# Ten more no-ops ahead of the second long visit of TensorE's stream, four fewer ahead of the fifth, and TensorE's idle operand cleared as VectorE's first instruction

## The chip, the cores and the metric

The kernel runs on one core of a Trainium2 chip. Times are device microseconds of one execution of the whole kernel, medians over several runs. A profile's "span" is shorter by about 2 us, since it counts only from the first to the last of the program's own instructions.

## The reference, cut to what matters

```python
x = A_x                                   # 2048 x 512, bf16
xn = _layernorm(x)                        # per row
# sliding-window attention: 32 heads of 16, window of 256 keys
# (qkv projection, scores, softmax, values, output projection)
attn = _A_ref(xn, A_wqkv, A_wo)
# bilinear gated unit, width 1792
glu = ((xn @ w_gate) * (xn @ w_up)) @ w_down
return x + attn + glu
```

## The kernel before

TensorE does nearly all of it in one stream that was ordered by hand: big matmuls of 512 columns ("filler": projections, gate, up, down) stand between small groups for the attention. A score group multiplies 32-row pieces of K and Q. A values group multiplies many small pieces of the probabilities with V; where two such groups follow each other, the text speaks of a "long visit". There are five of them, of 384 instructions each (192 weight loads and 192 matmuls).

Three pieces of the kernel matter here. The start, where VectorE clears an operand on which TensorE then idles, to get its clock up before the real work comes:

```python
# ... the DMA issues of x and of the weights stand above
warm = const.tile([128, 1], F32, name="warm")
nc.vector.memset(warm[:], 0.0)
nc.scalar.activation(out=warm[:], in_=warm[:], func=ACT.Exp)
self.idle = const.tile([128, 128], BF16, name="idle")
nc.vector.memset(self.idle[:], 0.0)
self.keep_busy(40)              # 40 matmuls idle x idle, result unused
```

The stock of no-ops, which is filled at given steps and used up three at a time:

```python
PADS = {27: 110, 57: 150}       # step: no-ops added to the stock
# ... in run(), at each step g
self.pads += PADS.get(g, 0)
# ... in fill(), after each piece of filler (two matmuls of 512 columns)
for _ in range(min(3, self.pads)):
    self.nc.tensor.nop("pad", nofuse=True)
    self.pads -= 1
```

And the values group:

```python
for i, (P, col, m, q, n) in enumerate(todo):
    for par in range(2):
        for e in range(4):
            # ... v is a 64 x 32 piece of V or of its half-swapped copy VS
            nc.tensor.matmul(accs[par][32 * e:32 * e + 32, q:q + n], lhsT=v,
                             rhs=P[rows, e, col:col + n], ...)
```

The softmax here doesn't subtract the row's maximum and nothing guards it: scores larger than these inputs give would overflow.

## Time and profile before

| | before |
|---|---|
| time, median of the first 3 runs | 263.57 us (263.21 to 263.72) |
| time, median of the 6 runs known later | 263.34 us (263.21 to 263.72) |
| span of the profiled execution | 261.2 us |
| TensorE's share of the chain that ended last | 98% |
| each of the five long visits in that chain | 2.40 us |
| first idle matmul, first projection matmul | 1.07 us, 6.67 us |

How to read it: TensorE's share of the chain says which engine sets the end, and the lengths of equal pieces of work say whether that engine is ever held up. The lines themselves stand in the prediction.

### The profile page before, as it was taken

The page shows a single profiled execution, that of the slowest core. Times are in us where ns is not written, and L with a number is a line of the kernel's source. Part 1 is how long each engine was busy: PE and PEld are TensorE (multiplying, and loading weights), DVE is VectorE, ACT ScalarE, POOL GpSimd, SP SyncE. Part 2 cuts the span into 40 slices and gives each one's busy share as a digit, 9 for nine tenths or more (in the row PEclk, how much of TensorE's full clock was granted, in tenths as well). Part 3 has the DMA queues.
Part 4 walks back from the last instruction along what each step waited for, and adds up shares of the span by engine and source line. Part 5 has one row for each costly group of instructions (what it writes and reads, how often), then busy time and mean ns, then how long its engine had stood idle before and what let it go on. Part 6 is the DMA issues. An engine that isn't in the chain of part 4 may idle for free.

```text
span 261.2 us, 7718 instructions
## 1 busy us (share of the span) xinstructions
PE 255.8 (98%) x3154; PEld 118.0 (45%) x3170; DVE 179.5 (69%) x357; ACT 176.4 (68%) x143; POOL 116.0 (44%) x278
## 2 busy tenths in 40 slices
PE   8999999999999999999999999999999999999995
PEld 8444444444344544444544454344544445444453
DVE  6787888779846597557974769767795235977344
ACT  3477688888757776678775567767787546787600
POOL 6225342425457644333457644544443451464600
PEclk9999999999999999999999999999999999999999
DMA  6999910120012300002001310001000100000002
GB/s 193 379 350 341 286 30 20 24 48 1 3 37 46 83 3 1 3 0 48 3 3 40 84 43 3 0 1 29 23 3 0 42 24 20 5 0 3 1 3 83
DMA packets 19427, 15.05 MB, mean 58 GB/s; under 512 B 7360, under 2 KB 19392, under 8 KB 19392
## 3 DMA queue, kind: packets, MB, share of 16 engines
q1 hardware_dynamic: 18848, 14.26, 18.6%
q8 instruction: 26, 0.43, 0.7%
q10 hardware_dynamic: 544, 0.30, 0.4%
q14 instruction: 9, 0.07, 0.1%
HBM read 9.70 MB, written 2.10 MB: 45 GB/s over the span
## 4 chain that ended last, share of the span: by engine, by line
PE 98%; issue 1%; DVE 0%
PE gp L399 19%; PE up L410 19%; PE psd L432 17%; PE qkp L255 11%; PE S L317 10%; PE acc L370 7%; PE vp L243 5%; PE psd L438 5%; PE L L432 2%; PE wps L131 2%; PE L L438 1%; PE xTp L213 0%; PE L L370 0%; DVE x L448 0%; DVE idle L95 0%
## 5 line engine op out<-in xcount | busy, mean ns | idle before, releaser
L323 ACT ACTIVATE P<-S 128x2048 bf16<-128x2048 f32 x75 | 140.7, 1876 | 49.6 <-PE S L317 41.0
L162 POOL TENSOR_SCALAR_AFFINE_SELECT P<-P 64x256 bf16<-64x256 bf16 x224 | 99.7, 445 | 123.7 <-ACT P L323 108.6
L399 PE MATMUL gp<-xnT,Wg 128*128 128x512 bf16 x224 | 60.1, 380 | 0.0
L410 PE MATMUL up<-xnT,Wu 128*128 128x512 bf16 x224 | 59.1, 380 | 0.0
L415 DVE TENSOR_TENSOR hT<-up,gsb 128x512 bf16<-128x512 f32 x56 | 38.3, 684 | 18.3 <-PE up L410 13.1
L432 PE MATMUL psd<-Wd,hT 128*128 128x512 bf16 (+1 forms) x202 | 46.9, 369 | 0.8 <-issue 0.6
L347 DVE TENSOR_TENSOR P<-P,diag 128x512 bf16<-128x512 bf16 (+1 forms) x75 | 29.6, 394 | 5.9 <-ACT P L323 5.9
L432 PEld LDWEIGHTS <-hT 128*128 128x128 bf16 x238 | 21.3, 98 | 25.3 <-issue 3.5
L410 PEld LDWEIGHTS <-Wu 128*128 128x128 bf16 x224 | 20.4, 98 | 25.6 <-issue 3.3
L399 PEld LDWEIGHTS <-Wg 128*128 128x128 bf16 x224 | 20.3, 98 | 25.3 <-issue 3.3
L317 PE MATMUL S<-Q,K 32*128 32x320 bf16 (+4 forms) x720 | 29.8, 254 | 0.1
L255 PE MATMUL qkp<-xnT,Wqkv 128*128 128x512 bf16 x128 | 29.9, 380 | 0.0
L234 ACT ACTIVATE gsb<-gp 128x512 bf16<-128x512 f32 x38 | 22.3, 596 | 7.7 <-PE gp L399 6.9
L317 PEld LDWEIGHTS <-K 32*128 32x128 bf16 x720 | 10.3, 92 | 30.7 <-issue 30.3
L376 DVE STREAM_TRANSPOSE at<-acc 128x512 f32<-128x512 f32 x30 | 19.1, 688 | 6.5 <-PE acc L370 6.4
L448 DVE TENSOR_TENSOR x<-psd,x 128x512 bf16<-128x512 f32 (+1 forms) x15 | 9.7, 655 | 15.7 <-PE psd L438 15.7
L255 PEld LDWEIGHTS <-Wqkv 128*128 128x128 bf16 x128 | 11.7, 98 | 14.7 <-issue 1.8
L370 PE MATMUL acc<-P,VS 64*32 64x320 bf16 (+4 forms) x672 | 17.7, 253 | 0.0
L370 PE MATMUL acc<-P,V 64*32 64x320 bf16 (+4 forms) x672 | 17.5, 253 | 0.0
L370 PEld LDWEIGHTS <-V 64*32 64x32 bf16 x720 | 15.1, 91 | 2.3 <-issue 1.7
L243 PE MATMUL vp<-Wqkv,xnT 128*128 128x512 bf16 x60 | 14.9, 380 | 0.3 <-issue 0.2
L370 PEld LDWEIGHTS <-VS 64*32 64x32 bf16 x720 | 14.7, 91 | 0.6 <-issue 0.2
(54 smaller groups left out, 180.5 us busy)
## 6 DMA issues: line engine op xcount, KB each, us to landing
out_dram<-x SPq DMA_DIRECT2D x15, 128.0 KB, 1.8
Wg<-in_B_w_gate_dram SPq DMA_DIRECT2D x2, 896.0 KB, 11.2
Wu<-in_B_w_up_dram SPq DMA_DIRECT2D x2, 896.0 KB, 12.6
Wd<-in_B_w_down_dram SPq DMA_DIRECT2D x1, 1792.0 KB, 17.4
Wqkv<-in_A_wqkv_dram SPq DMA_DIRECT2D x3, 512.0 KB, 6.3
x<-in_A_x_dram SPq DMA_DIRECT2D x2, 512.0 KB, 8.6
VS<-V SPq DMA_DIRECT2D x6, 144.0 KB, 2.6
x<-in_A_x_dram SPq DMA_DIRECT2D x3, 256.0 KB, 4.8
```

Of the source, the lines that this page charges most:

```text
L162: nc.gpsimd.affine_select(out=v, in_=v, pattern=pattern + [[1 if diag else -1, 64]], compare_op=ALU.is_ge if diag else ALU.is_gt, fill=0.0 ...
L234: nc.scalar.activation(out=out, in_=in_, func=ACT.Copy)
L243: nc.tensor.matmul(ps[:], lhsT=self.xnT[T][:, b, k, :], rhs=self.Wqkv[:, k, 1024:1536], start=(k == 0), stop=(k == 3))
L255: nc.tensor.matmul(ps[:], lhsT=self.Wqkv[:, k, lo:lo + 128], rhs=self.xnT[T][:, :, k, :], start=(k == 0), stop=(k == 3))
L317: nc.tensor.matmul(S[:, e, col:col + n], lhsT=self.K[U, c][rows, keys], rhs=self.Q[T, c][rows, q:q + n], start=True, stop=True, tile_posit ...
L323: nc.scalar.activation(out=P[:, :, 0:col], in_=S[:, :, 0:col], func=ACT.Exp, scale=0.25)
L347: self.nc.vector.tensor_tensor(out=v, in0=v, op=ALU.min, in1=self.diag.unsqueeze(1).unsqueeze(1).to_broadcast([128, 4, n, 64]))
L370: nc.tensor.matmul(accs[par][32 * e:32 * e + 32, q:q + n], lhsT=v, rhs=P[rows, e, col:col + n], start=(i == 0), stop=(i == len(todo) - 1), ...
L399: nc.tensor.matmul(ps[:], lhsT=self.Wg[:, k, 128 * f:128 * f + 128], rhs=self.xnT[T][:, :, k, :], start=(k == 0), stop=(k == 3))
L410: nc.tensor.matmul(ps[:], lhsT=self.Wu[:, k, 128 * f:128 * f + 128], rhs=self.xnT[T][:, :, k, :], start=(k == 0), stop=(k == 3))
L415: nc.vector.tensor_tensor(out=self.hT[T, f][:], in0=ps[:], in1=self.gsb[:], op=ALU.mult)
L432: nc.tensor.matmul(ps, lhsT=self.hT[T, f][:, 128 * b:128 * b + 128], rhs=self.Wd[:, f, c0:c1], start=(f == 0), stop=False)
```

## The change

The intent: TensorE's instructions are fetched in blocks (in the trace of the kernel before, the instruction queue carried 26 packets of 16,384 bytes for a program of 6609 instructions), and a visit uses them up far faster than filler does (160 against 9 per us). The no-ops move the visits against the block boundaries. Clearing the idle operand first lets TensorE start a little earlier. The whole diff, without its context:

```diff
-PADS = {27: 110, 57: 150}
+PADS = {27: 120, 57: 146}
@@ setup @@
+        self.idle = const.tile([128, 128], BF16, name="idle")
+        nc.vector.memset(self.idle[:], 0.0)
+        self.keep_busy(40)
         warm = const.tile([128, 1], F32, name="warm")
         nc.vector.memset(warm[:], 0.0)
         nc.scalar.activation(out=warm[:], in_=warm[:], func=ACT.Exp)
-        self.idle = const.tile([128, 128], BF16, name="idle")
-        nc.vector.memset(self.idle[:], 0.0)
-        self.keep_busy(40)
```

## The prediction

> **What bounds the kernel now.** I read four views: the page, the chain of work that ended last (whole and in windows), the waits of TensorE, and the first microseconds of the timeline. The page first:
>
> ```profile
> span 261.2 us, 7718 instructions
> PE 255.8 (98%) x3154; PEld 118.0 (45%) x3170; DVE 179.5 (69%) x357; ACT 176.4 (68%) x143; POOL 116.0 (44%) x278
> ...
> q8 instruction: 26, 0.43, 0.7%
> ...
> PE 98%; issue 1%; DVE 0%
> ```
>
> The chain is TensorE from end to end. A busy TensorE can still be a slow one, so I asked whether its stream has holes. The waits of TensorE are all of these:
>
> ```profile
> PE wps L131 <- DVE idle L95: 1.1, 1, 1.1
> PE psd L432 <- issue: 0.6, 4, 0.2
> PE L L432 <- issue: 0.2, 1, 0.2
> PE psd L438 <- issue: 0.2, 1, 0.2
> PE vp L243 <- issue: 0.2, 1, 0.2
> ```
>
> The first is the start. The others are 0.2 us each. I take them for lost records, not waits: the page counts 3170 weight loads and 3154 matmuls, and in the records each such place shows one step of about 432 ns, twice the usual 216 ns. Listing the start-to-start steps of all matmuls after 10 us gives only five kinds for the big ones: 216 ns between matmuls of 512 columns, 312 ns going into a score group, 227 ns coming out of one, 200 to 237 ns at the edges of a values group, and the doubled ones. So from about 9 us on the array streams at its own pace with no hole.
>
> The parts that the change aims at are the "long visits": two groups of values matmuls in a row, 384 instructions, of which this chain's pieces hold the first and the fourth:
>
> ```profile
> 88.72 0.33 PE S L317 x8
> 89.05 2.40 PE acc L370 x175
> 91.45 0.33 PE S L317 x8
> ...
> 185.53 0.33 PE S L317 x8
> 185.86 2.40 PE acc L370 x175
> 188.26 0.33 PE S L317 x8
> ```
>
> All five (they start at 89.05, 123.33, 154.17, 185.86 and 220.15) last 2.40 us in the chain. That is 384 / 2.40 = 160 instructions per us, against 2 / 0.216 = 9 per us elsewhere. If an instruction fetch came too late in one of them, that one would be longer than the rest; none is.
>
> [...]queue 8 has 26 packets of 16,384 bytes, 26 x 256 = 6656 instructions, and the built program of TensorE has 6609. [...]the 260 no-ops stand with the sequencer, no matmul step gets longer among them, and inside a group of three they start 71 ns apart. [...]Here full clock was granted 6.27 us after the span's start, 5.2 us after the first matmul, and the steps fell from 107 ns to 56 ns there.
>
> **Part 1, the no-ops.** Three no-ops follow each piece of filler work until the stock is used up. The change makes the first stock 120 in place of 110 and the second 146 in place of 150: six more in all, 6615 instructions on TensorE. The order of instructions against the kernel before shows that nothing else moves on any engine but the two memsets; only numbers in tile names change.
> - Cost: 6 x 71 ns = 0.43 us of the sequencer. It is hidden if the sequencer is ahead. Comparing each no-op's place in the program with the weight load that starts at that time, the sequencer is 5 to 41 instructions ahead of the array, median 25, and among the no-ops the array has no hole. A piece of filler is two matmuls, 432 ns, beside 3 x 71 = 213 ns of no-ops. So 0 us.
> - Aim: the no-ops move the visits against the 256-instruction blocks. Counting in the program and taking the remainder by 256, the visits begin at 28, 202, 234, 18 and 232 before, and at 28, 212, 244, 28 and 238 after. Reading 18 and 28 as 274 and 284 on a circle, all the old places lie in 202 to 284, and so do all the new ones. Every old place shows 2.40 us, the fourth visit takes exactly the place of the first, and the other new places lie between places that are good. The fetches near the visits agree: the shortest spacing of two starts is 3.38 us (187.74 and 191.12), and each took 0.9 to 1.4 us in that part. So nothing to gain, nothing to lose: 0 us.
>
> **Part 2, the memsets.** The start, from the timeline:
>
> ```profile
> 0.86 0.06 DVE L92 MEMSET warm<- 128x1 f32 x1 [0.86 <-PEq L659]
> 0.90 0.11 DVE L95 MEMSET idle<- 128x64 uint32 x1
> 1.07 4.45 PE L131 MATMUL wps<-idle 128*128 128x128 bf16 x40 [1.07 <-DVE idle L95]
> ...
> 2.08 0.20 ACT L93 ACTIVATE warm<-warm 128x1 f32<-128x1 f32 x1
> ...
> 5.96 0.41 DVE L194 TENSOR_SCALAR xn<-x,mv,rs 128x512 bf16<-128x512 bf16 x1
> ...
> 6.43 0.23 PEld L213 LDWEIGHTS <-xn 128*128 128x128 bf16 x4
> ```
>
> Cleared first, the idle operand is ready 0.90 - 0.86 = 0.04 us earlier, so the first idle matmul starts at about 1.03 in place of 1.07. ACT's warm-up comes after its table load at 2.08 and isn't touched. The idle matmuls only warm the clock: the first real work waits for the norms. The first transposes may gain up to 0.04 us, since the last idle matmul starts at 5.21, about when their operand is ready (4.80 + 0.38 = 5.18). The next transposes wait for a tile that VectorE ends at 5.96 + 0.41 = 6.37, and the first projection stands behind them, so those 0.04 us are absorbed. Sum of both parts: 0 to 0.04 us gained of 263.57.
>
> **The rivals.**
> - A fetch stall hidden in the timed runs: [...]one of the three timed runs (263.21 to 263.72) could hold a stall that the profile hasn't. For it: somebody chose these numbers of no-ops. Against it: the profiled execution took 263.23, near the fastest timed run, so at most 263.57 - 263.21 = 0.4 us can be won. It would give about 263.2.
> - A new stall: a new place could make a visit cross two blocks before the second has arrived. A fetch takes up to 1.4 us here; estimated from that, a stall costs 0.5 us in each visit and 4 x 0.5 = 2 us at worst, 265.6. Against it: the bracketed places above. I give it one in twenty, for one visit rather than four.
> - [...]Estimated from the steps, a late grant makes the first four or so projection matmuls 0.2 us longer each, 0.8 us. That is noise of both kernels, and probably most of the 0.5 us between the three runs.[...]
> - The extra no-ops bind after all: 0.43 us, 264.0. Against it: the 5 to 41 instructions of lead.
>
> **Range and chances.** The middle is 263.57 less 0.04, and a little less for the first rival: 263.45 us. The range must hold the spread of the runs (0.5 us) and the first and third rivals below, the fourth above: 263.0 to 264.0. Two per cent is 5.3 us, over twice the worst rival; I leave 1% on each side for what I haven't seen. The real question here is tenths of a microsecond, and my answer is no difference beyond noise.
>
> **What would show it right or wrong.** In the changed profile the five long visits should be 2.40 us each, no-ops 266 on TensorE's sequencer with no matmul step over 312 ns besides lost records, the first idle matmul near 1.03 us, the first transposes of the second tile still near 6.43 us, and TensorE busy near 255.8 us. A visit longer than 2.40 us, or a step of over 0.4 us near a block fetch, would prove the second rival; five visits shorter than 2.40 us would show that all five were stalled before, which I can't tell from equal lengths alone. A full-clock grant away from 6.27 us with a span moved by as much would prove the third.

Passages that no trace or run of this case bears out are cut from the recorded text, and the cuts are marked. None is a term of its sum, which is 263.57 us, less 0.04 for the memsets, a little less for the first rival: 263.45 us. The third rival, the late grant of full clock: 0.8 us, an estimate from the measured steps; these fell from 107 to 56 ns at the grant, so a matmul of 216 ns would take about 0.2 us more before it.

## The result, and the profile after

The changed kernel took 263.38 us (median of 6 runs, 263.17 to 263.52), the kernel before 263.34 us in its 6 runs. The ratio is 0.9999, with a 95% interval of 0.9986 to 1.0011. Ratios here and below are the mean time of one kernel's fast runs over that of the other's of the same rounds, so they are not quite the ratio of the medians that are quoted.

The page of the changed kernel, its span and its busy times:

```profile
span 261.3 us, 7724 instructions
...
PE 255.5 (98%) x3154; PEld 117.4 (45%) x3170; DVE 179.5 (69%) x357; ACT 176.4 (67%) x143; POOL 115.7 (44%) x278
```

There are 6 more instructions, the no-ops, and the busy time of TensorE is the same to 0.3 us. From the chain of work that ended last, the piece with the fourth visit (start in us, length in us, what):

```profile
185.67 0.33 PE S L317 x8
186.00 2.40 PE acc L370 x175
188.40 0.33 PE S L317 x8
```

As before, this visit lasts 2.40 us, and so do the other four. It only starts 0.14 us later (186.00 against 185.86). Where those 0.14 us come from shows at the start. The timeline of the changed kernel's first microseconds (start, length, engine, line, operation, result and sources, and in brackets the idle time before with what ended it):

```profile
0.87 0.11 DVE L92 MEMSET idle<- 128x64 uint32 x1 [0.87 <-PEq L659]
0.93 0.06 DVE L95 MEMSET warm<- 128x1 f32 x1
1.04 4.15 PE L131 MATMUL wps<-idle 128*128 128x128 bf16 x40 [1.04 <-DVE warm L95]
...
6.42 0.23 PEld L213 LDWEIGHTS <-xn 128*128 128x128 bf16 x4 [0.51 <-DVE xn L194]
...
6.79 1.02 PE L243 MATMUL vp<-Wqkv,xnT 128*128 128x512 bf16 x3
```

The profile names `warm` as what TensorE waited for, since that memset ended last (0.99 us); in the program TensorE waits for the first memset alone, that of `idle`, which ended at 0.98. The first idle matmul starts at 1.04 in place of 1.07, so the second part does what it was made for. The second tile's transposes begin at 6.42, where they began before at 6.43. But the first projection matmul starts at 6.79, and before it was 6.67. The records show why: TensorE's sequencer has a wait instruction ahead of that matmul, for the landing of the first third of the projection weights. It ended at 6.50 us before and at 6.69 us after. A transfer that landed 0.2 us later took away more than the memset gave, and neither is visible in the times.

The waits of TensorE show the early clock in another way:

```profile
PE wps L131 <- DVE warm L95: 1.0, 1, 1.0
...
PE xTp L213 <- DVE xn L194: 0.3, 1, 0.3
```

The second line is new. In this execution full clock was granted at 4.74 us (6.27 before), so the 40 idle matmuls were done sooner (4.15 us in place of 4.45), and TensorE then waited 0.3 us for the norm. The clock came 1.5 us earlier and nothing was won by it.

### The profile page after: what moved, and what is told of

Same layout as the page of the kernel before. It is cut to its first block, busy times and chain, and to the rows that moved or that the text cites. A ratio compares the mean times of both kernels' runs of the same rounds, so it can differ in the third digit from the quotient of the medians.

```text
span 261.3 us, 7724 instructions
## 1 busy us (share of the span) xinstructions
PE 255.5 (98%) x3154; PEld 117.4 (45%) x3170; DVE 179.5 (69%) x357; ACT 176.4 (67%) x143; POOL 115.7 (44%) x278
## 4 chain that ended last, share of the span: by engine, by line
PE 96%; DVE 1%; DMA 1%; issue 1%
PE gp L399 19%; PE up L410 19%; PE psd L432 17%; PE qkp L255 11%; PE S L317 10%; PE acc L370 7%; PE vp L243 5%; PE psd L438 5%; PE L L432 2%; DMA x<-in_A_x_dram 1%; DVE st L173 1%; PE L L438 1%; PE L L370 0%; PE xTp L213 0%; DVE xn L194 0%
```

## The experiments

Ten more kernels were run, all of them correct. "Place" of a visit means: the number of its first instruction in TensorE's program, modulo 256. The prediction lists the five places of both kernels.

My theory was that both parts are off the path: the stream of TensorE has no holes, so no-ops can't fill any, and the start waits for other things than the idle operand. The first rival was that the two parts have effects that cancel. The second was that the no-ops do nothing at all, wherever a visit lies.

### The two parts alone

e1 has only the new no-op counts, e2 only the new order of memsets.

```diff
 e1: -PADS = {27: 110, 57: 150}
     +PADS = {27: 120, 57: 146}      (memsets as before)
 e2: the memset hunk of the change   (PADS as before)
```

> Only the no-op counts of the change (120 and 146), with the old order of the two memsets. Theory (both parts are off the path): ratio to the kernel before 1.000 within 0.001, the five long visits 2.40 us each. Rival (the no-ops gain and the memsets lose, or the reverse, and they cancel): a ratio off by over 0.001 here, about 0.3 us, and off by as much the other way in the run with the memsets alone.

> Only the idle operand cleared first, with the old no-op counts (110 and 150). Theory: ratio 1.000 within 0.001; the first idle matmul about 0.03 us earlier than before, and the first projection matmul no earlier than 6.6 us, since it waits for the norms of the second tile and for the landing of its weights. Rival (parts cancel): off by over 0.001, opposite to the run with the no-ops alone.

Measured: e1 263.35 us, ratio 0.9997 (0.9985 to 1.0009). e2 263.47 us, ratio 1.0002 (0.9990 to 1.0014). Neither differs from the kernel before, and all visits are 2.40 us. The intervals are a little wider than the thousandth that I asked for, so two effects of up to 0.4 us that cancel are not excluded by the times alone. The traces are finer. In the records of five profiles (times in us), from the first projection matmul to the first matmul of the first visit, and from there to the first matmul of the fifth visit:

| profile | first idle matmul | full clock granted | wait for the weights ends | first projection | first visit | from projection to first visit | from first to fifth visit |
|---|---|---|---|---|---|---|---|
| before | 1.072 | 6.27 | 6.502 | 6.670 | 88.978 | 82.31 | 131.10 |
| after | 1.040 | 4.74 | 6.685 | 6.792 | 89.112 | 82.32 | 131.10 |
| e1, no-ops alone | 1.071 | 4.74 | 6.407 | 6.581 | 88.897 | 82.32 | 131.10 |
| e2, memset alone | 1.039 | 5.78 | 6.687 | 6.794 | 89.113 | 82.32 | 131.10 |
| e8, idle start late (below) | 2.149 | 6.30 | 6.645 | 6.751 | 89.061 | 82.31 | 131.10 |

The last two columns are the same to 0.01 us. The no-ops stand between 93.9 and 214.2 us, so it is the last one that tests them. From the first projection to the last matmul it is 251.65 to 251.67 us in all five; what differs between executions lies before the first projection, or after the last matmul (2.86 to 3.02 us). Where the wait for the weights ended after 6.6 us, the projection follows it by 0.107 us in every row; where it ended earlier, it follows the second tile's transposes. It follows neither the first idle matmul nor the clock's grant.

### No no-ops at all

```diff
-PADS = {27: 120, 57: 146}
+PADS = {}
```

> The changed kernel without any no-op. The five long visits then begin at 28, 92, 124, 164 and 228 of their 256-instruction blocks. Theory (a visit that crosses two block boundaries waits for a fetch): visits two, three and four get longer than 2.40 us by 0.3 to 0.9 us each (about 1 us from crossing to fetch and about 1.1 us of fetch, less the 1.6 us in which a visit runs through 256 instructions), the first and the fifth stay at 2.40; in all 1 to 2.7 us more, 264.4 to 266. Rival ([...]the place of a visit doesn't matter and the no-ops do nothing): all visits 2.40 us and 263.4.

Measured: 270.57 us, ratio 1.0241 (1.0201 to 1.0282), single runs from 267.84 to 271.95. So the no-ops are worth 6 to 7 us (by the ratio of the fast runs, or by the medians), and the second rival falls. The chain of this run around its second visit, at place 92:

```profile
123.54 2.25 PE acc L370 x161
125.79 2.05 issue
127.84 0.40 PE acc L370 x13
```

In the middle of the visit TensorE does nothing for 2.05 us, and nothing that the profile knows holds it ("issue"). The third and fourth visits (places 124 and 164) have such a hole each; the first and the fifth (28 and 228) have none. In the program all three holes lie at the same place: before the instructions 3010, 3778 and 4546, each 194 modulo 256. I take that for where a block begins. The packets of the instruction queue, read from the packed trace, agree. In the second visit a block was entered at 123.99 us, the next fetch ran from 124.98 to 126.43, and the hole ended at 127.84. Over the three holes, a fetch starts 0.8 to 1.0 us after a block is entered, it takes 1.2 to 1.45 us, and the hole ends about 1.4 us after the fetch has ended. That makes about 3.7 us (3.5 to 3.85) from one boundary to the next at the least in this run. At 160 instructions per us the visit needs only 1.6 us for 256 instructions. The difference, 2.1 us, is the hole. Expected were 0.3 to 0.9 us, because I had left out the 1.4 us after the fetch.

The holes were not all. Of the windows of this run, one starts with the fourth visit, the next follows it (columns: busy us of TensorE, its weight loads, VectorE, ScalarE, GpSimd, then the granted clock and the DMA engines):

```profile
190.00:195.00 5.00, 3.09 (x208) 2.36 (x208) 2.19 (x6) 2.37 (x2) 1.64 (x4) 1.00 0.02 5
195.00:198.40 3.40, 3.40 (x13) 1.15 (x10) 2.58 (x6) 1.88 (x1) 0.82 (x2) 0.52 0.03 5
```

In the 3.4 us after the hole, which lasted 1.91 us, the granted clock was 0.52, and eight matmuls took 427 ns each in place of 216: 1.7 us more. After the two earlier holes, of 2.05 and 1.78 us in the chain, there was no such stretch; what decides it stays open. This profile counts as slow, as its run was over 1.5% above the fastest of its kernel. I don't rest the holes on it alone: of the fast runs, the two at a granted clock of 0.999 and 1.000 took 268.4 and 267.8 us, so with next to no time at a cut clock the loss is still over 4 us (267.8 against 263.4), and e5 and e6 below show holes at a granted clock of 1.000.

### The same no-ops in bursts

```diff
-                for _ in range(min(3, self.pads)):
+                for _ in range(min(12, self.pads)):
```

> The changed kernel with the same 266 no-ops, up to twelve after each piece of filler in place of three. A group then takes the sequencer 12 x 71 = 852 ns beside two matmuls of 432 ns. Theory (no-ops are hidden by the sequencer's lead of 5 to 43 instructions only while they come slowly): holes of 0.2 to 0.5 us appear in the matmul stream near most of the 22 groups, 3 to 9 us more, 266 to 272. Rival (no-ops cost the array nothing however they come): no holes and 263.4.

Measured: 270.76 us, ratio 1.0279 (1.0264 to 1.0294). The places of the visits are those of the changed kernel, and every visit is 2.40 us. The loss is now in the filler, as the waits of TensorE show:

```profile
PE up L410 <- issue: 1.9, 6, 0.4
PE psd L432 <- issue: 1.4, 6, 0.5
PE gp L399 <- issue: 1.3, 4, 0.4
```

Near a burst the step between two matmuls is mostly 650 to 750 ns in place of 216, and each is one hole of about 0.45 us. So the same no-ops that cost nothing in threes cost 7 us in twelves. At 71 ns from one to the next, three per piece of filler take 213 ns of the sequencer beside 432 ns of the array; twelve would take 852 ns, and the first long step comes at 96.4 us, 2.4 us after the first no-op.

### Where a visit may lie

e5 and e6 place the five visits elsewhere by other counts of no-ops, to find both edges of the good range.

```diff
-PADS = {27: 120, 57: 146}
+PADS = {8: 10, 27: 76, 37: 94, 57: 34}     (e5)
+PADS = {8: 20, 27: 58, 37: 82, 57: 28}     (e6)
```

> Other counts of no-ops, so that the five long visits begin at 38, 178, 48, 88 and 186 of their blocks (counted in the program, modulo 256). In the run without no-ops all three holes fell at instruction 194 modulo 256, and block fetches there came every 3.8 to 4.0 us. Theory (a boundary can be passed only some 3.7 us after the one before it, while a visit runs 160 instructions per us; what the array still holds at its slow pace of 108 ns per instruction hides the rest): holes of about 0.4 us (38), 0.6 us (178), 1.5 us (48), 1.9 us (88) and none (186). Rival (any visit which a boundary enters after its first instructions is held for the same 2 us, by the number of boundaries inside alone): 38 and 48 have one boundary inside and get no hole, 88 gets 2 us, and 178 and 186, with two inside, get 2 us as well.

> As the run before, with the visits at 48, 170, 28, 68 and 160. Theory: holes of about 1.5 us (48), 1.4 us (170), none (28), 1.9 us (68) and 2 us (160). Rival (number of boundaries inside alone): none at 48, none at 28, none at 68 (its second boundary lies two instructions before the end, so at most a short hole), 2 us at 170 and 160.

Measured: 266.70 and 268.26 us. Each is one run and so of unknown state, but at a granted clock of 1.000; the argument rests on places within one profile. The chain of e5 from its third visit on:

```profile
154.59 2.40 PE acc L370 x175
...
157.64 1.15 issue
...
187.61 2.26 PE acc L370 x164
189.87 1.46 issue
```

The third visit (place 48) is itself whole; its hole comes after it, in the filler. The fourth (88) has it inside. In e6 the first visit lies at 48:

```profile
91.83 0.33 PE S L317 x8
92.16 0.32 PE up L410
92.48 1.04 issue
```

Here the score group after the visit and one matmul still run, then the boundary holds TensorE. All places together; the time lost is taken from the records, as the length from first to last matmul start of the visit less the usual 2.20 us, or as the long step after it less 216 ns:

| place | time lost, us | seen in |
|---|---|---|
| 160, 164 | 1.4, 2.1 | e6, e3 |
| 170, 178 | 0.32, 0.27 | e6, e5 |
| 186 | 0 | e5 |
| 202 to 244 | 0 | before, after, e3 |
| 18, 28 | 0 | before, after, e3, e6 |
| 38 | 0.16 | e5 |
| 48 | 1.3, 1.2 | e5, e6 |
| 68, 88 | 1.7, 1.7 | e6, e5 |
| 92, 124 | 2.3, 1.9 | e3, e3 |

The good range goes from about 186 round to about 28. The rival, which counts only the boundaries inside the visit, falls: place 48 has one boundary inside and loses 1.2 us, 178 has two and loses 0.27. My sizes were too large near the edges: 0.6 for 178, 1.4 for 170, 2 for 160 and 0.4 for 38. At the low edge the array has more left to run than I had reckoned: in e5 the fetch at the first boundary of the visit at 178 started at 122.75 us, 0.7 us before the array came to that boundary (123.44), so the sequencer had crossed it well ahead.

### The start

e7 leaves the 40 idle matmuls out. e8 clears the idle operand about 1.1 us later. No-ops in the first chunk keep all visits in their places.

```diff
 e7: -        self.keep_busy(40)
     -PADS = {27: 120, 57: 146}
     +PADS = {8: 80, 27: 120, 57: 146}
 e8: idle tile, its memset and keep_busy(29) moved below the three small constants of VectorE
     +PADS = {8: 22, 27: 120, 57: 146}
```

> The changed kernel without the 40 idle matmuls ahead of the first norms, so TensorE starts cold at about 5.2 us; 80 no-ops in the first chunk keep all later instructions at the same places in their blocks. Theory (the idle matmuls only buy the clock; the first projection waits for norms and weights in any case): [...]the first two or three tiles' projections run at 427 ns per matmul, 0.3 to 2 us more, 263.7 to 265.4. Rival (start of TensorE is irrelevant altogether): 263.4.

> The changed kernel with the idle operand cleared after the other small constants of VectorE, so TensorE's first idle matmul starts at about 2.1 us in place of 1.04; 29 idle matmuls in place of 40, so that they still end by 5.2 us, and 22 no-ops in the first chunk keep later instructions in their places. Theory (over 25 times the shift that the change makes has at most a small effect[...]): ratio within 0.001 of the kernel before, 263.3 to 263.7. Rival (an earlier start of TensorE is worth its time in full): 0.0117 us per 0.01 us, so about 1 us more, 264.4.

(e7: the 0.3 to 2 us was my estimate. The rival's "0.0117 us per 0.01 us" for e8 is a slip. Its 264.4 follows from 1.1 us lost in full.)

Measured: e7 264.83 us, ratio 1.0065 (1.0039 to 1.0092). e8 263.33 us, ratio 0.9999 (0.9986 to 1.0011). The timeline of e7 shows the first two tiles' projections (line 242 here):

```profile
6.87 1.92 PE L242 MATMUL vp<-Wqkv,xnT 128*128 128x512 bf16 x4
9.00 1.11 PE L242 MATMUL vp<-Wqkv,xnT 128*128 128x512 bf16 x4
```

Without idle matmuls full clock came at 9.16 us, and the first tile's projection ran cold, 1.92 us in place of some 1.03. So the idle matmuls are worth 1.5 us in all. But starting them earlier is worth nothing here. In the chain of e8

```profile
2.15 3.28 PE wps L131 x29
...
6.80 0.98 PE vp L243 x4
```

they start 1.1 us later than in the changed kernel, and the projection is where it was. That is over thirty times the shift that the change makes, and it costs nothing that the runs can see. In these runs a grant of full clock at 6.30 us (e8) was early enough, and one at 9.16 us (e7) was not.

### Could the start be made shorter?

The weights' landing seemed to be worth moving. e9 loads their first third from ScalarE's queue at 0.8 us; e10 also puts the first tile's projection ahead of the second tile's transposes.

```diff
 e9:  -            nc.sync.dma_start(out=self.Wqkv[...], in_=wq[...])
      +            (nc.scalar if lo == 1024 else nc.sync).dma_start(out=self.Wqkv[...], in_=wq[...])
 e10: the same, and
      +            if b == 0:
      +                self.proj_v(0, engine="dve")
                   if b < 3:
                       self.norm_transpose(b + 1, False)
      -            self.proj_v(b, engine="act" if b == 2 else "dve")
      +            if b:
      +                self.proj_v(b, engine="act" if b == 2 else "dve")
```

> The changed kernel with the first third of the projection weights loaded from ScalarE's queue at about 0.8 us, in place of the fourth transfer of SyncE's queue at 2.2 us. In the changed kernel's trace TensorE waited until 6.69 us for that load, and the first projection matmul started at 6.79 us; with the load early it can start at about 6.66, straight after the second tile's transposes. Theory (the landing of those weights, not the clearing of the idle operand, sets the tenths at the start): first projection matmul 6.60 to 6.70 us, ratio 0.9995, about 0.1 us gained, too little to be clear. Rival (the early load takes the transfer engines from the x tiles, so the norms come later): first norm after 2.97 us and 0.2 to 1 us lost.

> As the run before, and the first tile's projection stands ahead of the second tile's transposes. Theory (TensorE has a hole between the warm-up and the second tile's norm, which the first projection can fill once its weights are there): first projection matmul near 6.2 us, 0.2 to 0.4 us gained, ratio 0.9985 to 0.999. Rival (the norms of tiles three and four set the end of the start in any case, so the work is only moved): ratio 1.000 within 0.0005.

Measured: e9 266.18 us, ratio 1.0101 (1.0088 to 1.0114). e10 265.14 us, ratio 1.0066 (1.0049 to 1.0083). Both are slower. For e9 the direction is its rival's, but 2.7 us is more than the 0.2 to 1 us that it gave; for e10 both expectations missed. VectorE's statistics of the first two tiles in e9:

```profile
3.26 0.69 DVE L173 BATCH_NORM_STATS2 st<-x 128x6 f32<-128x512 bf16 x1 [1.25 <-DMA x<-in_A_x_dram]
...
5.85 0.69 DVE L173 BATCH_NORM_STATS2 st<-x 128x6 f32<-128x512 bf16 x1 [1.49 <-DMA x<-in_A_x_dram]
```

The second tile's statistics started at 5.85 us; in the kernel before, at 3.99. With the weights' transfer early, the x tiles landed later: this one took 4.59 us in the chain of e9. The first projection came at 8.80 us, 2.0 us later than in the changed kernel. Full clock came at 10.13 us in place of 4.74, so part of the first projections ran at a lower clock (in the chain of e9 two matmuls took 0.84 us, 0.42 us each in place of 0.216), and from there to the first visit it took 82.98 us in place of 82.32. The two together are the 2.7 us. In e10 full clock came at 9.97 us, but its profile is of one of its two slowest runs (266.37). The order of transfers that both kernels have is better than these two, and no experiment points to a version that beats them.

## Why the prediction was right

**The bound and the absence of holes: right.** TensorE's stream in both kernels is the same to 0.01 us, over the 82 us ahead of the no-ops and over the 131.10 us that hold all of them. What was taken for lost records is just that: the profiles of e5 and e6 hold 3170 matmuls in place of 3154, and there TensorE has none of these waits of 0.2 us for "issue".

**The no-ops' cost: right.** Six more cost nothing, as the sequencer was 5 to 41 instructions ahead in the trace of the kernel before. e4 shows the limit of that argument: the same no-ops in twelves cost 7 us.

**The no-ops' aim: right in the outcome, by the places.** The new places lie between good ones, and e3, e5 and e6 show that the good range really is one piece from about 186 to about 28. But the step that set the spacing of two fetches (3.38 us) against the time of one (0.9 to 1.4 us) failed: it reads as 2 us of margin, and there is none. In e3, e5 and e6 the fetches on either side of a hole start 3.4 to 4.0 us apart, with 2.3 to 2.6 us from the end of one to the start of the next. At the fourth visit of the kernel before, where 3.38 us was read, it is 2.3 us too (188.81 to 191.12), at its first visit 2.6, and at both of them in the changed kernel 2.5. So near the first and fourth visit both kernels fetch about as fast as the runs did around their holes. What margin there is I take for the slow filler (9 instructions per us) that the array still has to do meanwhile. Measured in places, the change moves the second visit from 16 to 26 above the good place 186, and the fourth from 18 to 28, where the next place tried, 38, already loses 0.16 us. I had not seen that the change goes away from one edge and towards the other.

**The memsets: right, with a cause missing.** 0.03 us earlier (0.04 predicted), all of it absorbed. The prediction said that the first real work waits for the norms; it waits for the norms and for the weights' landing, whichever is later, and in three of the five profiles it was the weights.

**The rivals.** A hidden stall, worth up to 0.4 us, falls: the median did not move. A new stall was put at 0.5 us in each visit; where the visits were moved outside the edges it measured 1.2 to 2.3 us (0.16 to 0.32 close to them), and one hole of e3 was followed by 3.4 us at a granted clock of 0.52. The term that was missing is the time after the fetch, 1.4 us. The rival of no-ops that bind is true only in bursts. A late grant of full clock was called the likely source of most of the 0.5 us between runs: full clock came anywhere from 4.74 to 6.30 us in the table above and the time didn't follow. In the nine profiles that share this start, or differ from it only in when the idle matmuls begin (all but e7, e9 and e10), the first projection came anywhere from 6.58 to 7.05 us, after the weights' landing or the norms. That is about as wide as the spread of the timed runs and its likely source, but the timed runs have no traces, so it is not shown.

**The number.** 263.45 predicted, 263.38 measured, and all six runs lie inside 263.0 to 264.0. The starting point, 263.57, was the median of three runs and stood 0.23 us above that of six. So the closeness is partly luck: the 0.12 us that the middle lay below it did not come from the change.

## What to carry to other kernels

Where an engine's stream has fast stretches (here 160 instructions per us against 9, and 1.2 to 2.3 us lost by most visits in a bad place), ask where the instruction blocks begin in them: measure the time from one block's boundary to the next in a run that has a hole, and place the fast stretch so that enough slow work lies between two boundaries. Once no hole is left, moving it further gains nothing, and it can only come nearer to the other edge (here the change took the fourth visit from 18 to 28, both without loss, and 38 lost 0.16 us). An operand that is ready earlier is worth something only if the work behind it is the last to be waited for (in e8 an idle operand 1.1 us later cost nothing), so look at what the first real instruction waits for before tuning the warm-up.
